# The carried state of four early units, run chunk by chunk through its own copy, and a new order for the words around it

## The chip, the cores and the metric

The kernel runs on one core of a Trainium2 chip. The metric is the device time of one execution in microseconds. Times are the medians of several runs; a trace is of one profiled execution, whose own time stands beside its span below.

## The reference

Two parts follow each other. The first is a gated linear attention: for each of 4 batches and 8 heads a state of 48x48 runs over 768 steps.

```python
for t in range(S):
    state = alpha[:, :, t, :, None] * state + np.einsum('bhd,bhe->bhde', k[:, :, t], v[:, :, t])
    y[:, :, t] = np.einsum('bhd,bhde->bhe', q[:, :, t], state)
```

The second takes y as rows `x` of 3072 tokens by 384 and computes `silu(x @ w_gate) * (x @ w_val) @ w_out` with 1536 inner columns. The weights come in as doubles and are cut and split on the chip into a high and a low single-precision part.

## The kernel before, in words

The attention is cut into 16 **units** of 192 steps (`T`), four to a batch; units 0 to 3 are batch 0. A unit has 3 **chunks** of 64 steps (`NU`, `C`), and its 8 heads lie as 4 pairs (`G`), one head of a pair in partitions 0 to 63 and one in 64 to 127. The second part is cut into **steps**: block of 384 tokens by 128 inner columns. Step s has three products of nine matmuls each: `g` (gate, PSUM bank `gps`), `v` (value, bank `vps`) and `o` (output, three banks).

Everything is written as **words** in one table, `ORDER`. A word is `engine:name@banks`, with engines t (TensorE), v (VectorE, DVE), s (ScalarE, ACT), g (GpSimd, POOL) and y (the DMA queue of SP). Each engine carries out its words in the order of the table and waits where a word needs something that is not ready; nothing else orders the work. Digits after @ name the PSUM banks that the word writes.

The words of one unit u, as far as the change and the prediction speak of them:

- `La`, `Lq`, `Lk`, `V u.i`: loads of alpha, q, k and v. `pa`, `pq`, `pk` copy a load to a wide tile, `Ta`, `Tq`, `Tk` transpose it on TensorE, and `ea`, `cq`, `ek` copy it out of PSUM.
- `G`, `f`, `mk`, `q`: the scans over alpha and the products with k and q. `qc` copies a part of q's product.
- `K u.c` transposes a chunk of keys, `kc u.c` copies it into the tile `K` (two copies a chunk on ACT, lines 514 and 515).
- `S`: the scores (line 551), `ma u.i`: their masked copies. `Y`: the output of the unit (lines 629 to 646). `yh`, `yl` split it, `R u.k` rearranges it on TensorE and `x u.k` copies it to `xT`, from which step products read.
- `vc u`: a copy of v to the tile `U` for the second half of `Y`.
- `Bw u` (units 0 to 3) or `B u` (later units), function `carry`: what each chunk adds to the state. `ad u.c`, function `advance`: the state before the next chunk, written into free rows of the v tile `V`; for the last chunk it goes to `SE`. `de u`: VectorE multiplies `SE` by the decay and makes it the state ahead of the next unit's first chunk.

For the early units `Bw` makes whole sums: the state after chunk c is a sum of the products of chunks 0 to c, so that chunk 0 is multiplied once, twice and three times; the tile `K` holds an identity in the state rows of chunk 0, which brings in the state ahead of the unit. All three sums can then be made one after another with no copy between them.

Weights have words of their own: `wl p` (load), `w p v0` to `v2` (cut, ACT or DVE), `w p a` (high part) and `w p p` (low part). `sl s`, `h s`, `hh s`, `hl s` are the silu and the product between the matmuls of a step, `sl` on ACT. `first` is one 1x1 silu without any other use.

Of the kernel before, what the change touches and what calls it, by code (L numbers as in the profile page):

```python
# [48 lines left out]
s:pa2 y:V1.5 g:w1a v:w1p s:w4v0 y:La3 s:pa3 g:q1 v:de1 t:S1@62 t:Bw1@3 s:ad1.0 v:w2v2 g:w2a y:Lq2 v:w3v2 v:yl0.0
v:yl0.1 t:R0.1@7 g:qc1 v:ma1.0 v:ma1.1 v:w4v1 v:ma1.2 t:Ta2@05 s:ea2 v:G2 s:ad1.2 g:vc1 t:Y1@41 s:yh1.0 v:yl1.0  # L50
s:yh1.1 v:yl1.1 t:R0.0@2 s:x0.0 s:x0.1 y:Lk3 t:Ta3@35 y:Lk2 s:pk2 t:R0.2@6 v:w4v2 g:pq2 t:Tq2@04 s:cq2 v:lm1 t:R1.2@1
s:x1.2 s:x0.2 t:Tk2@72 v:mk2 t:R1.0@4 s:x1.0 v:f2 v:q2 t:R1.1@0 s:x1.1 t:K2.0@2 s:kc2.0 s:w4a v:w4p t:K2.1@7 s:kc2.1
s:w3a v:w3p g:w2p t:g0 s:sl0 t:K2.2@1 g:pk3 t:Tk3@40 s:ea3 v:G3 y:wl5 s:w5v0 v:w5v1 y:V2.3 y:V2.2 y:V3.1 y:V3.0
y:V3.3 y:V2.4 y:Lq3 s:pq3 y:V2.5 y:V2.1 y:wl7 y:V2.0 y:wl10 t:S2@27 t:g1 s:sl1 s:kc2.2 t:v0 v:h0 s:hh0 g:hl0 y:wl6
y:V3.2 y:V3.5 t:g2 s:vc2 t:Tq3@51 s:cq3 s:w7v0 s:sl2 g:lm0 y:La4 v:de2 t:Bw2@3 s:ad2.2 s:ad2.0 t:v1 v:mk3 v:ma2.2
t:K3.1@4 s:kc3.1 y:wl9 v:f3 v:q3 t:S3@16 s:w6v0 t:K3.0@3 s:kc3.0 g:qc2 v:ma2.0 v:ma2.1 t:Y2@42 s:yh2.0 y:V3.4 y:wl8
v:w5v2 s:w5a v:de3 t:Bw3@0 s:ad3.0 s:yh2.1 v:h1 s:hh1 v:w6v1 v:w6v2 v:yl2.0 v:ma3.2 g:qc3 v:ma3.0 v:yl2.1 y:wl12
y:wl11 y:xr2.0 y:Lk4 y:wl13 y:xr2.1 s:w6a v:w6p t:v2 v:h2 v:ma3.1 t:o0 g:w5p t:g3 t:v3 v:w7v1 s:w9v0 s:hh2 v:hl2
g:hl1 t:o1 t:o2 v:w7v2 s:w8v0 s:vc3 y:wl14 v:w8v1 t:K3.2@1 v:w9v1 v:w8v2 s:sl3 v:h3 s:w7a v:w7p v:w9v2 s:w8a v:w8p
s:w10v0 v:w10v1 s:w9a v:w9p t:Y3@20 s:yh3.0 t:g4 s:sl4 s:hh3 g:hl3 s:yh3.1 v:yl3.1 t:v4 v:h4 v:yl3.0 y:xr3.1 y:xr3.0  # L60
y:xr3.2 y:xr2.2 y:wl16 t:g5 s:w11v0 v:w11v1 v:w10v2 t:v5 s:sl5 v:h5 s:hh4 v:hl4 v:w11v2 s:w10a v:w10p t:o3 t:o4
s:w12v0 v:w12v1 s:hh5 v:hl5 v:w12v2 s:w11a v:w11p s:w12a g:w12p v:tk4 t:g6 t:v6 s:sl6 v:h6 s:hh6 g:hl6 v:tr4 v:G4
y:V5.2 y:Lq4 y:V4.2 t:o5 t:g7 s:sl7 s:kc3.2 s:w13v0 t:v7 v:h7 t:o6 s:ot6.1 y:V4.4 y:os6.1 s:ot6.0 y:os6.0 y:La5 v:mk4
v:w13v1 v:f4 s:w14v0 s:hh7 g:hl7 y:wl15 y:V5.0 y:V4.1 y:V4.0 y:wl17 t:g8 s:sl8 t:v8 v:h8 s:hh8 g:hl8 v:w14v1 t:g9
s:w16v0 v:tq4 s:ot6.2 s:sl9 t:v9 v:h9 v:w13v2 t:o7 v:w14v2 s:w14a g:w14p v:q4 v:tr5 t:g10 t:v10 s:sl10 y:V5.4 s:w13a
v:h10 s:hh10 v:kr4.2 v:kr4.0 t:o8 s:hh9 v:hl9 s:w15v0 v:w15v1 v:w13p v:w16v1 t:g11 t:v11 s:sl11 v:h11 t:o9 g:hl10
t:o10 v:w15v2 s:w15a s:hh11 g:hl11 v:G5 t:g12 t:v12 v:kr4.3 s:sl12 v:h12 s:w17v0 s:hh12 t:g13 s:sl13 v:w16v2 g:hl12
t:v13 t:o11 t:o12 y:Lk5 y:os6.2 v:tk5 g:mk5 v:w15p v:kr4.1 v:h13 s:hh13 y:V4.5 y:V4.3 y:Lq5 g:hl13 s:qc4 s:w16a v:f5
t:g14 v:tq5 g:q5 g:w16p v:w17v1 y:wl18 s:sl14 t:v14 v:h14 s:hh14 g:hl14 t:S4@21 v:ma4.2 t:B4@0 v:ma4.1 v:kr5.0 t:o13
s:ot13.0 s:ot13.1 s:vc4 v:kr5.1 y:os13.0 s:ad4.0 v:ad4.1 v:ma4.0 t:g15 s:sl15 t:v15 v:h15 s:w18v0 v:w18v1 t:g16  # L70
s:sl16 s:ot13.2 s:hh15 g:hl15 v:w17v2 s:w17a g:w17p v:w18v2 s:w18a g:w18p t:v16 v:h16 v:ad4.2 y:La6 v:tr6 t:g17 t:v17
s:sl17 v:h17 t:o14 t:o15 y:V5.1 y:Lk6 v:tk6 v:kr5.2 s:hh17 g:hl17 v:kr5.3 t:Y4@56 s:yh4.0 s:yh4.1 v:yl4.0 v:yl4.1
y:V5.3 y:V5.5 v:G6 v:mk6 t:S5@10 t:B5@2 v:kr6.2 v:kr6.1 t:g18 s:sl18 t:v18 t:g19 s:hh16 g:hl16 t:o16 t:o17 y:Lq6
# [1036 lines left out]
```

## Time and profile before

| | |
|---|---|
| median of 3 runs | 553.8 us (553.6 to 554.41) |
| profiled execution | 553.2 us, span 551.5 us |
| TensorE busy | 537.0 us (97%) |
| VectorE busy | 383.9 us (70%) |
| ScalarE busy | 257.7 us (47%) |
| GpSimd busy | 134.4 us (24%) |

Busy time on TensorE (PE in the rows) is the time in which a matmul is under way. Idle time of another engine costs nothing unless TensorE or the last store waits for it. The shares are means over the whole span; the change lies in its first third, where ScalarE and VectorE are much fuller than these means.

### The profile page before, as it was taken

Reading aid. Unit: us, or ns where it says so; the run is one execution under the profiler, and the core shown is the slowest. Engines: PE = TensorE matmul, PEld = TensorE weight load, DVE = VectorE, ACT = ScalarE, POOL = GpSimd, SP = SyncE. Lnnn points to the kernel's source line nnn. Section 1 sums busy time; section 2 is a strip of 40 time slices with the busy share of each in tenths; the row PEclk is TensorE's granted clock in tenths of the full one; section 3 lists DMA queues with packets and bytes.
Section 4 is the critical chain, followed back from the end, with each engine's and each line's share of the span. In section 5 each row is a group of like instructions: output and inputs, shape, how many; then the busy total and the mean of one; then the engine's idle time right before and its main releaser. Section 6 shows DMA issues by size and latency. Waiting matters only on the chain.

```text
span 551.5 us, 13702 instructions
## 1 busy us (share of the span) xinstructions
PE 537.0 (97%) x5510; PEld 524.5 (95%) x5510; DVE 383.9 (70%) x612; ACT 257.7 (47%) x581; POOL 134.4 (24%) x146
## 2 busy tenths in 40 slices
PE   5999999999999999999999999999999999999996
...
GB/s 253 192 233 283 250 153 256 139 81 152 166 155 217 142 125 161 82 112 86 102 106 188 142 73 171 145 86 159 74 168 36 65 40 91 84 125 115 131 174 115
DMA packets 95362, 77.61 MB, mean 141 GB/s; under 512 B 32832, under 2 KB 92224, under 8 KB 95296
## 3 DMA queue, kind: packets, MB, share of 16 engines
...
q10 hardware_dynamic: 288, 0.39, 0.2%
...
## 4 chain that ended last, share of the span: by engine, by line
PE 87%; DVE 4%; SPq 3%; ACT 2%; DMA 2%; issue 2%; DVEq 0%; ACTq 0%
PE v L715 25%; PE g L715 25%; PE ops L747 24%; PE A L575 3%; PE y L646 2%; PE s L551 2%; PE pt L416 1%; PE y L629 1%; SPq L700 1%; DMA Le<-in_k_dram 1%; PE y L630 1%; PE kps L510 1%; DMA L<-in_k_dram 1%; DVE Gs L460 1%; DVE K L526 1%
## 5 line engine op out<-in xcount | busy, mean ns | idle before, releaser
L715 PE MATMUL g<-xT,w 128*128 128x384 f32 x864 | 167.5, 337 | 0.6 <-issue 0.6
L715 PE MATMUL v<-xT,w 128*128 128x384 f32 x864 | 166.8, 337 | 0.3 <-DVE h L727 0.3
L747 PE MATMUL ops<-w,hh 128*128 128x384 f32 x576 | 157.3, 336 | 0.0
L715 PEld LDWEIGHTS g<-xT,w 128*128 128x128 f32 x864 | 150.9, 188 | 1.9 <-issue 0.9
L715 PEld LDWEIGHTS v<-xT,w 128*128 128x128 f32 x864 | 150.9, 188 | 1.4 <-DVE h L727 0.8
L736 POOL TENSOR_TENSOR hl<-h,hh 128x384 fp32r<-128x384 f32 x63 | 67.5, 1073 | 309.5 <-ACT hh L731 279.5
L727 DVE TENSOR_TENSOR h<-h,v 128x384 f32<-128x384 f32 x96 | 53.1, 553 | 103.3 <-PE v L715 94.5
L731 ACT CAST hh<-h 128x384 fp32r<-128x384 f32 x96 | 49.0, 513 | 141.4 <-DVE h L727 69.5
L747 PEld LDWEIGHTS ops<-w,hh 128*128 128x128 f32 x576 | 105.3, 188 | 0.2
L747 PE MATMUL ops<-w,hl 128*128 128x384 f32 x288 | 96.8, 336 | 0.0
L723 ACT ACTIVATE h<-g 128x384 f32<-128x384 f32 x96 | 47.0, 490 | 77.4 <-PE g L715 66.5
L526 DVE STREAM_TRANSPOSE K<-Gs 32x384 f32<-32x384 f32 x96 | 54.7, 570 | 1.9
L747 PEld LDWEIGHTS ops<-w,hl 128*128 128x128 f32 x288 | 54.1, 188 | 0.1
L736 DVE TENSOR_TENSOR hl<-h,hh 128x384 fp32r<-128x384 f32 x33 | 18.8, 575 | 24.0 <-ACT hh L731 23.9
L469 DVE TENSOR_TENSOR_SCAN AT<-AT,back 128x771 f32<-128x771 f32 x16 | 32.6, 2037 | 0.6
L585 DVE TENSOR_TENSOR X<-s,mask 64x384 f32<-64x384 f32 (+1 forms) x48 | 26.1, 552 | 6.2 <-PE s L575 3.2
L460 DVE TENSOR_TENSOR_SCAN Gs<-AT,inj 128x772 f32<-128x772 f32 x16 | 28.8, 1803 | 0.4 <-ACT AT L811 0.2
L660 ACT CAST X<-y 112x384 fp32r<-112x384 f32 x28 | 12.5, 478 | 32.3 <-PE y L646 26.5
L664 DVE TENSOR_TENSOR X<-y,X 112x384 fp32r<-112x384 f32 x28 | 15.2, 552 | 14.1 <-ACT X L660 13.9
L317 ACT ACTIVATE wc<-wc,wbias 128x384 f32<-128x384 f32 x36 | 23.3, 648 | 1.2
L575 PE MATMUL A<-V,K 64*48 64x48 f32 (+1 forms) x720 | 22.0, 207 | 1.8 <-issue 1.8
L575 PEld LDWEIGHTS A<-V,K 64*48 64x48 f32 (+1 forms) x720 | 19.4, 123 | 2.6 <-issue 1.8
...
## 6 DMA issues: line engine op xcount, KB each, us to landing
...
```

The lines of the kernel that those rows point to most:

```text
L317: nc.scalar.activation(dev, dev, AF.Relu, bias=wbias, scale=-1.0, accum_out=wviol[:, 0, i : i + 1])
L460: nc.vector.tensor_tensor_scan(*(x.rearrange("p g t -> p (g t)")[:, ::-1] for x in (Gs, AT, inj)), 0.0, op0=ALU.mult, op1=ALU.add)
L469: nc.vector.tensor_tensor_scan(Af, Af, back[:, 1 : n + 1], back[:, 0:1], op0=ALU.mult, op1=ALU.add)
L526: nc.vector.transpose(out=bass.AP(k0.tensor, k0.offset, [k0.ap[0], (G * 2 * D, NU), (2 * D, G), (1, 32)]), in_=Kg[j * BO + x : j * BO + x ...
L575: nc.tensor.matmul(to[j * BO : j * BO + D, g - gs.start, :], Ks[r, x, g, KC[j]], Vd[r, x, g, VC[j]], start=(x == 0 or not whole), stop=(x ...
L585: nc.vector.tensor_tensor(out=X[r, z, f * GF : (f + 1) * GF, :].rearrange("r g (c t) -> r g c t", c=NU), in0=sps[f][r].rearrange("r g (c t ...
L715: nc.tensor.matmul(pt, wsp[kind, f][a][:, kt * P : (kt + 1) * P], xT[blk][:, b_, kt, :], start=(n == 0), stop=(n == 3 * KT - 1),)
L723: nc.scalar.activation(h, acc.pop(("g", blk, f)), AF.Silu)
L727: nc.vector.tensor_tensor(out=h, in0=h, in1=acc.pop(("v", blk, f)), op=ALU.mult)
L731: nc.scalar.copy(out=hh, in_=acc["h", blk, f])
L736: eng.tensor_tensor(out=hl, in0=acc.pop(("h", blk, f)), in1=hh.bitcast(F32), op=ALU.subtract)
L747: nc.tensor.matmul(ops[blk][i], h[b_][:, i * P : (i + 1) * P], wsp["o", f][a], start=(first and n == 0), stop=(last and n == 2),)
```

## The change

`Bw` is gone. In its place stand three words `C u.c` a unit (two for unit 3), function `running`: one product per pair and half, 8 a chunk. The tile `K` now holds the identity in the state rows of every chunk, so the product of chunk c takes the state from the rows where `ad u.(c-1)` has put it. `ad u.c` is now a word for every chunk (in the table before, `ad u.0` copied two chunks at once). A unit has 24 products where it had 48.

```diff
-            nc.gpsimd.tensor_copy(out=t_[r, 0, :, KC[j]], in_=ident[r, r].unsqueeze(1).to_broadcast([D, G, D]))
+            nc.gpsimd.tensor_copy(out=t_[r, :, :, KC[j]], in_=ident[r, r].unsqueeze(1).unsqueeze(1).to_broadcast([D, NU, G, D]))
...
+    def running(u, c, bank):
+        st = state[u]
+        Ks, Vd = st["K"], st["V"]
+        st["sum"] = ps.tile([P, G, D], F32, tag=bank, name=f"A2_{u}_{c}")
+        for g in range(G):
+            for j in range(2):
+                r = slice((1 - j) * BO, (1 - j) * BO + C) if c == 0 and first_of_batch(u) else slice(0, P)
+                nc.tensor.matmul(
+                    st["sum"][j * BO : j * BO + D, g, :], Ks[r, c, g, KC[j]], Vd[r, c, g, VC[j]], start=True, stop=True
+                )
...
     def advance(u, c, eng):
...
+        if "sum" in st:
+            for j in range(2):
+                r = slice(j * BO, j * BO + D)
+                to = Vd[r, c + 1, :, VC[j]] if c + 1 < NU else SE[r]
+                (eng.copy if eng is nc.scalar else eng.tensor_copy)(out=to, in_=st["sum"][r])
+            return
...
-        todo[f"Bw{u}"] = lambda eng, bank: carry(u, bank, True)
+        for c in range(NU):
+            todo[f"C{u}.{c}"] = lambda eng, bank, c=c: running(u, c, bank)
```

The table `ORDER` is new down to word `h25` (some 640 words); from there both tables agree. Its first line of old and of new:

```diff
-s:first y:La0 y:wl0 s:pa0 t:Ta0@20 s:ea0 y:La1 s:pa1 y:Lq0 s:pq0 y:Lk1 y:Lk0 t:Ta1@67 s:pk0 v:w0v0 v:w0v1 v:w0v2 s:w0a g:w0p
+y:La0 v:pa0 t:Ta0@53 s:ea0 y:wl0 v:w0v0 v:w0v1 v:w0v2 y:Lq0 s:pq0 v:G0 v:f0 t:Tq0@41 v:q0 y:La1 s:pa1 y:Lk1 s:pk1
```

Besides the order, some words change engine. Ahead of step 0, ACT gains `qc0`, `w1a` and `w2a` (POOL had them) and gives `w2v0`, `pa0` and `pa2` to DVE; `w3a` now stands ahead of the last `x` copies of unit 1 and `w4a` behind the first silu, where both stood between those copies and the silu. After it ACT gains `qc2`, `qc3` and `pk3` and gives `w7v0` and `w10v0` to DVE, while DVE gives `w6p` and `w9p` to POOL. `first` moves from the head of ACT's words to far behind the first silu.

**TensorE, unit 1.** Before, the words S1, Bw1 and R0.1 stand together (s_1 is the scores' tile, A_1 and a part of s_1 take the state sums, xp is unit 0's rearranged output):

```order
L551 MATMUL s_1_446<-X_103,Gs_212 64x64 x2
L551 MATMUL s_1_447<-X_103,Gs_212 64x64 x2
L575 MATMUL A_1_472<-V_81,K_104 48x48 x24
L575 MATMUL s_1_446<-V_81,K_104 48x48 x12
L575 MATMUL A_1_472<-V_81,K_104 48x48 x12
L686 MATMUL xp_1_531<-Y_428,sel_121 128x384 x2
```

In the changed kernel the same place reads (A_1_0, A_1_1 and A_1_2 are the sums of the three chunks; the rows of S1 are left out, and y_1 is the word Y1):

```order
L589 MATMUL A_1_0_410<-V_81,K_104 48x48 x8
L417 MATMUL pt_0_0_434<-ident,wide 128x128 x3
L417 MATMUL pt_0_1_438<-ident,wide 128x128 x3
...
L589 MATMUL A_1_1_472<-V_81,K_104 48x48 x8
L589 MATMUL A_1_2_487<-V_81,K_104 48x48 x8
L648 MATMUL y_1_512<-X_103,V_81 64x64
```

48 products have become 3 times 8, and the last two groups stand side by side with nothing between them, though the third needs ACT's copy of the second.

**ScalarE around the first silu.** Before (kps are key transposes, t3 and t4 cut weights, h0_0 the silu of step 0):

```order
L514 COPY K0_104<-kps2_1_670 64x4x48
L515 COPY K0_104<-kps2_1_670 64x4x48
L340 CAST w3_677<-t3_276 128x768
L723 ACTIVATE h0_0_691<-g0_0_681 128x384
L811 COPY AT_85<-pt3_0_0_606 128x4x32x3
L811 COPY AT_85<-pt3_0_1_610 128x4x32x3
L160 ACTIVATE t5_714<-raw5_711,lbias_119 128x768
L404 COPY wide_82<-L1_72 128x12x48
L723 ACTIVATE h0_1_770<-g0_1_760 128x384
```

And in the changed kernel:

```order
L516 COPY K0_104<-kps2_1_644 64x4x48
L742 ACT_TABLE_LOAD
L742 ACTIVATE h0_0_664<-g0_0_654 128x384
L341 CAST w4_669<-t4_502 128x768
L830 COPY AT_85<-pt3_0_0_565 128x4x32x3
L830 COPY AT_85<-pt3_0_1_569 128x4x32x3
L492 COPY X0_102<-X0_102 48x384
L515 COPY K0_104<-kps2_2_679 64x4x48
L516 COPY K0_104<-kps2_2_679 64x4x48
L405 COPY wide_82<-L1_72 128x12x48
L161 ACTIVATE t5_700<-raw5_589,lbias_119 128x768
L742 ACTIVATE h0_1_702<-g0_1_686 128x384
```

A table load has come in ahead of the first silu, and between the silus of steps 0 and 1 stand three more words: `w4a` (line 341), `qc2` (492) and `kc2.2` (515 and 516). In both programs one more table load stands at the very head of ACT's work.

## Rows read from the trace of the kernel before

**Rows 1.** The page: busy us, share, instructions; TensorE's busy tenths in 40 slices
```profile
PE 537.0 (97%) x5510; PEld 524.5 (95%) x5510; DVE 383.9 (70%) x612; ACT 257.7 (47%) x581; POOL 134.4 (24%) x146
...
PE   5999999999999999999999999999999999999996
```

**Rows 2.** Stretches A:B: length, then busy us of PE, PEld, DVE, ACT, POOL; granted clock
```profile
5.00:10.00 5.00, 3.53 (x16) 3.16 (x17) 4.16 (x6) 2.37 (x5) 3.90 (x8) 1.00 0.99 304
...
20.00:25.00 5.00, 4.21 (x142) 3.46 (x142) 4.94 (x10) 4.81 (x14) 1.94 (x2) 1.00 0.79 193
25.00:30.00 5.00, 4.43 (x134) 4.10 (x137) 3.59 (x7) 4.24 (x10) 2.57 (x6) 1.00 0.69 184
30.00:35.00 5.00, 5.00 (x68) 4.44 (x61) 4.72 (x9) 4.86 (x13) 2.85 (x2) 1.00 0.77 199
```

**Rows 3.** Chain that ended last, 34 to 66 us: start, us, what
```profile
35.51 1.58 PE g L715 x9
...
37.47 0.66 PE pt L416 x6
38.13 0.86 PE s L551 x48
...
44.59 1.21 PE A L575 x48
45.80 0.54 PE s L575 x24
46.34 0.54 PE A L575 x24
...
52.08 1.22 PE A L575 x48
...
64.95 1.07 PE g L715 x5
```

**Rows 4.** Groups of instructions by shape: count, then busy us, mean ns
```profile
L340 ACT CAST w<-t 128x768 fp32r<-128x768 f32 x16 | 13.2, 834 | 10.5 <-DVE t L164 10.5
...
L491 ACT COPY X<-X 48x384 f32<-48x384 f32 x9 | 4.6, 510 | 0.2
...
L598 ACT COPY V<-A 48x384 f32<-48x384 f32 x8 | 3.8, 474 | 0.8 <-PE A L575 0.7
...
L404 ACT COPY wide<-L 128x576 f32<-128x576 f32 x5 | 3.4, 681 | 0.0
...
L160 ACT ACTIVATE t<-raw,lbias 128x384 f32<-128x384 uint32 x3 | 1.9, 647 | 0.0
L605 ACT COPY V<-A 48x192 f32<-48x192 f32 x6 | 1.9, 313 | 3.4 <-PE A L575 3.4
L605 ACT COPY SE<-A 48x96 f32<-48x96 f32 x6 | 1.4, 233 | 0.1
...
L340 ACT CAST w<-t 128x384 fp32r<-128x384 f32 x2 | 1.0, 511 | 2.8 <-DVE t L164 2.8
```

**Rows 5.** ScalarE in order of time: start, us, what [idle before <-releaser]
```profile
15.50 0.31 ACT L514 COPY K<-kps 64x192 f32<-64x192 f32 x1 [0.50 <-PE kps L510]
...
27.52 0.97 ACT L598 COPY V<-A 48x384 f32<-48x384 f32 x2 [0.66 <-PE A L575]
...
33.42 1.74 ACT L690 CAST xT<-xp 128x384 fp32r<-128x384 f32 x4
...
37.85 0.48 ACT L723 ACTIVATE h<-g 128x384 f32<-128x384 f32 x1
...
40.81 0.49 ACT L723 ACTIVATE h<-g 128x384 f32<-128x384 f32 x1 [0.17 <-PE g L715]
```

**Rows 6.** ScalarE, the first two instructions, same columns
```profile
0.91 1.28 ACT L897 ACT_TABLE_LOAD   x1 [0.91 <-PEq L1094]
2.20 0.20 ACT L897 ACTIVATE first<-one 1x1 f32<-1x1 f32 x1
```

**Rows 7.** TensorE in order of time, early transposes, same columns
```profile
7.98 2.82 PE L416 MATMUL pt<-ident,wide 128*128 128x128 f32 x12 [1.19 <-ACT wide L404]
```

More of the change, by code (lines that the diff above doesn't have):

```diff
@@ L49 @@
[L49 to L73, printed above, removed]
@@ new lines @@
+t:S0@24 t:K0.2@7 v:ma0.2 s:ek1 s:kc0.0 s:qc0 s:kc0.1 s:kc0.2 y:wl3 s:w3v0 y:V0.1 y:V0.3 y:V0.0 y:V1.4 y:V0.4 y:La2
+y:wl2 y:V0.2 y:V0.5 y:V1.3 y:Lq2 y:V1.1 t:Tq1@17 t:C0.0@6 v:mk1 v:w0p s:cq1 v:f1 g:q1 g:qc1 s:ad0.0 t:K1.0@0 t:K1.2@3
+s:kc1.0 t:C0.1@5 s:ad0.1 t:C0.2@6 t:K1.1@7 v:ma0.1 v:ma0.0 s:vc0 t:Y0@40 v:w2v0 v:pa2 y:V1.2 y:La3 y:V1.0 y:wl4 y:Lk3
+y:V1.5 s:ad0.2 v:de1 t:C1.0@2 s:kc1.2 s:kc1.1 s:yh0.0 s:yh0.1 v:w1v2 v:w2v1 s:ad1.0 v:w3v1 v:w2v2 s:w1a t:Ta2@31 s:ea2
+g:w1p v:w3v2 t:S1@57 t:C1.1@2 s:ad1.1 v:ma1.2 s:pa3 y:V2.0 y:V2.2 t:C1.2@7 y:V2.4 y:V2.1 y:Lk2 y:wl6 s:w4v0 s:w2a
@@ new lines @@
+s:ad1.2 v:ma1.1 v:ma1.0 g:vc1 t:Y1@61 s:yh1.0 g:pq2 s:yh1.1 v:yl0.1 v:yl0.0 t:R0.2@4 t:R0.0@2 s:x0.2 s:x0.0 t:Ta3@53
+s:pk2 t:Tq2@47 s:cq2 g:w2p y:V3.1 y:V3.0 y:V3.2 y:wl5 t:R0.1@2 s:x0.1 y:Lq3 y:wl9 y:V2.5 y:wl8 y:V2.3 v:G2 v:yl1.0
+v:yl1.1 v:w4v1 v:w4v2 t:R1.1@0 t:Tk2@47 v:mk2 s:x1.1 t:R1.2@6 v:f2 t:R1.0@2 s:w3a s:x1.2 s:x1.0 s:pk3 t:K2.0@4
+t:K2.1@7 s:kc2.0 s:kc2.1 v:q2 t:g0 s:sl0 v:de2 v:w3p s:w4a t:Tk3@17 t:K2.2@0 s:ea3 t:g1 s:qc2 s:kc2.2 s:pq3 s:w5v0
+s:sl1 y:wl7 y:V3.4 y:wl12 y:V3.3 y:V3.5 v:w4p v:G3 t:v0 v:h0 s:hh0 g:lm0 g:hl0 t:S2@02 t:C2.0@4 s:ad2.0 v:w5v1 v:ma2.2
@@ new lines @@
+v:mk3 t:g2 t:C2.1@1 s:sl2 s:ad2.1 t:Tq3@24 s:cq3 v:f3 v:q3 t:C2.2@7 s:ad2.2 t:K3.1@3 s:kc3.1 s:vc2 v:de3 v:ma2.0
+v:ma2.1 t:K3.0@6 s:kc3.0 t:v1 t:S3@17 t:C3.0@3 t:Y2@06 s:w6v0 s:ad3.0 s:qc3 v:w5v2 s:w5a g:w5p v:w6v1 v:h1 t:C3.1@2
+s:hh1 v:w6v2 s:w6a g:w6p s:yh2.0 s:yh2.1 s:vc3 v:ma3.2 v:lm1 v:ma3.1 v:w7v0 t:v2 v:hl1 t:o0 t:o1 v:h2 v:ma3.0 s:ad3.1
+t:Y3@21 y:wl11 y:wl13 y:V4.4 y:wl10 y:wl16 v:yl2.1 v:yl2.0 y:xr2.0 y:xr2.1 y:xr2.2 v:w7v1 v:w7v2 s:w9v0 s:w8v0 s:hh2
+v:w8v1 v:hl2 y:V4.2 y:Lk4 s:w7a t:g3 t:v3 t:o2 s:sl3 v:w8v2 v:w7p s:w8a t:g4 v:w9v1 v:h3 v:w9v2 s:w11v0 s:yh3.0
```

155 lines of the change are left out of this document (83 added, 72 removed).

## The prediction

> **What bounds the kernel now.** I read the page first. TensorE is busy 537.0 of the 551.5 us of the span, and its row of slices shows a 9 everywhere but in the first slice and the last [rows 1]. The kernel is a line of matmuls with a thin start; what is taken off TensorE there counts in full where the line is dense, and nothing where another engine sets the pace. So I looked at the start by stretches. From 20 to 30 us TensorE is busy 4.21 and 4.43 of each 5 us, from 30 on all 5.00; ScalarE in the same three stretches is busy 4.81, 4.24 and 4.86, VectorE 4.94, 3.59 and 4.72 [rows 2]. Up to about 35 us three engines are equally full, and a saving on TensorE alone need not arrive. The chain that ended last goes through matmuls alone from 35.51, the first step product, to 64.95, where g4 starts [rows 3]: there TensorE is the bound. ScalarE in order of time shows how units 0 and 1 end: the last four copies into xT, from which g0 reads, take 1.74 from 33.42 and end at 35.16 [rows 5]. The reader should see that g0 at 35.51 stands right behind both a full TensorE and a full ScalarE.
>
> **What the products save.** Bw2 is 96 records (a product leaves two) and takes 1.21 + 0.54 + 0.54 = 2.29 us; Bw3 is 48 records and takes 1.22 [rows 3]. The changed unit 2 has 48 records; at the price of the 48 of line 575 that is 1.21, in three groups of 0.40. Unit 3 has 32 records, 0.81. So units 0, 1 and 2 save 1.08 each and unit 3 saves 0.41, together 3.65 us of TensorE, 2.16 of it ahead of g0 and 1.49 behind it.
>
> **What the copies cost.** Before, ad of a unit is four copies of 48x96 to SE (0.233 each) and two of 48x384 (0.474): 1.88 us of ScalarE. After, it is six of 48x192 (0.313): 1.88 us [rows 4]. The copies are even; what changes is that each now stands between two products. GpSimd's wider identity copy at the start is before any product needs it and is costed at nothing; uncovered, it would be two copies of three times the size, some 1.5 us by ScalarE's 48x384 copy of 0.510 [rows 4].
>
> **Ahead of g0 (units 0 and 1).** Here I go by ScalarE, because its copies free the banks and fill the tiles. It gains qc0 (0.510), w1a and w2a (0.511 each) and w3a (0.834) ahead of the last xT copies, 2.37 us. It loses w2v0 (0.647) and pa2 (0.681), 1.33 [rows 4]. Net it has 1.04 more. In the old trace it idles 0.50 in front of the key copies at 15.50 and 0.66 in front of the state copies at 27.52 [rows 5], 1.16 in all. qc0 falls into the first gap. The second came from waiting for the end of Bw1; in the new order other words (w1a, then ea2; pa3, w4v0, w2a) stand between one state copy of unit 1 and the next, which are longer than the product of 0.40 with its own delay, so ScalarE doesn't wait. It ends the xT copies 0.12 earlier, near 35.0. TensorE does wait, between C1.1 and C1.2: the copy ad1.1 stands behind w1a (0.51) and ea2 (two copies of 128x384, by the pair at 27.52 some 0.97) and takes 0.63 itself, 2.11 in all, of which C1.1 covers 0.40 and S1 some more; about 1.2 us are left, half of the 2.16. The other half goes into waits for the state copies of unit 0. So this part gives -0.1 (bounds: -0.7 if ScalarE's gaps and a part of its overlap vanish, since TensorE then leads again; +1.5 if each of the unit's three state copies is late by half a microsecond).
>
> **Between g0 and g4 (units 2 and 3).** TensorE is dense, so 1.49 come off in full. Against it stand three new waits.
>
> First, the table load. `first` is moved behind the first silu, and the new ScalarE order has a load ahead of h0_0. Its row of before is 1.28 us [rows 6]. From 35.0 ScalarE has pk3 (0.681), four key copies (0.31 each by [rows 5]), the load and the silu (0.48): 35.0 + 0.68 + 1.24 + 1.28 + 0.48 = 38.7. g1 needs that silu, because it writes the bank that g0 filled. TensorE does g0 (1.58), Tk3 (0.66) and K2.2 (0.39) from 35.5 and is ready at 38.1 [rows 3]: a wait of 0.6 to 0.8; I take 0.7. Uncovered it would be 1.28, wholly covered 0.
>
> Second, the silu of step 1, on which g2 waits. Between the first two silus ScalarE took 40.81 - 37.85 = 2.96, with 0.17 of it idle [rows 5]. It now has w4a (0.834), qc2 (0.510) and kc2.2 (0.62) more: 2.79 + 1.96 = 4.75 from 38.2, so the silu ends at 43.4. TensorE does g1, v0 (1.57 each by g0's row), S2 (0.86) and C2.0 (0.40) from 38.8 and is ready at 43.2: 0.2 to 0.6, I take 0.4 (0 to 1.0).
>
> Third, unit 2's chunks: C2.2 waits for ad2.1, which waits for C2.1 and stands behind a silu of 0.49. Tq3 (0.66) covers most of it; 0.3 remains. In unit 3, Y2 and step products lie between the two groups, and I cost it at nothing; bare, one copy of two pieces (0.63) would show.
>
> Sum: -0.1 - 1.49 + 0.7 + 0.4 + 0.3 = **-0.2 us**. The profiled execution's span of 551.5 would become 551.3, its own time 553.2 become 553.0; the median of the runs stands 0.6 above that execution, so I forecast **553.6 us**.
>
> VectorE gains pa0, pa2, w0p, w2v0, w7v0 and hl1 and loses w1p, w6p and w9p up to g4. It had 1.41 us idle in 25 to 30 alone [rows 2], and I cost the difference at nothing; if that cover were gone, three casts of weights on the way to a step product would be late, which is part of the upper bound.
>
> **A rule of the skill on the table load.** The row at 0.91 is followed by its silu at 2.20, 0.01 behind the load's end: at the head of the program a load costs its own 1.28 and no more [rows 6].
> The Trainium skill (ScalarE: Activation LUTs, section What ACT_TABLE_LOAD costs) says that a switch of tables costs the load of about 1283 ns and on top of it a drain of about 1380 ns, 2.66 us together; the trace agrees on the load and, with nothing in front of it, shows no drain.
> By the row the sum is -0.2. By the page it would be an estimated +1.2, since g1 would wait 1.4 longer and little behind it could take that up.
>
> **The rivals.** Faster: the waits are covered, because matmuls start piece by piece as chunks get ready and ScalarE overlaps its ends. Then at least the 1.49 stay, at most all 3.65: 552.3 to 550.2, I would name 551.9. For it speaks that the old trace has hardly a wait on TensorE behind 30 us; against it that ScalarE is as full as TensorE there and that the load stands on its line. It decides when the first silu ends before 38.1.
>
> Slower: the load on ScalarE's line. A switch in the middle of the program must let the work in front of it end, and then both silus come later. If another length of the load is added, g1 waits 2.0, not 0.7: +1.1, 554.9, and 555.3 with the upper half of the other two waits. It decides when the first silu starts later than 39.0. For it: nothing stands between load and silu to cover it. Against: the old row shows 1.28 alone. The page of the Trainium skill named above (ScalarE: Activation LUTs, What ACT_TABLE_LOAD costs) would make it the likelier case.
>
> Slower too: TensorE's pace. The early transposes take 2.82 for 12 at 7.98, after an idle 1.19, and 0.66 for 6 at 37.47, at a granted clock that the rows give as 1.00, the 2.4 GHz level, from 5 to 10 us as from 20 on [rows 2, 3, 7]. If the new pauses bring that slow pace back for 5 us, the 4.21 us of work of the stretch from 20 to 25 would be half done, +2.1: 555.7. The pauses are shorter than 1.5 us each, so I give it little. That the change doesn't do what it says is out: the program has the 24 products.
>
> **How the numbers follow.** The forecast, saving and waits in balance (552.7 to 554.8): 0.47. Covered waits: 0.31. Longer load: 0.16. Pace: 0.06. Below 0.2% (1.1 us) this kernel's runs, which spread over 0.8, tell little. So faster 0.31, same 0.47, slower 0.22. The range reaches to the nearer part of the faster rival and through the load's: 551.8 to 555.2, which leaves about 0.1 on each side.
>
> **What would show it.** In the changed profile: 48 records of line 589 in unit 2 taking about 1.2; a load of 1.28 between the key copies and the first silu near 37, and g1 waiting for that silu by some 0.7; g2 for the next by 0.4; C1.2 waiting for a state copy by about 1; the first step product at 35.5. Wrong would be: g0 at 34 or at 37, a load of 2.6, or idle TensorE behind g4, which none of these terms has.

## The result: slower by about one per cent

The changed kernel takes 560.65 us (557.58 to 562.37, four runs) for 554.11 beside it, a ratio of 1.0112 with an interval of 1.0067 to 1.0158. Run again on another occasion it took 559.49 for 554.14, 1.0093 (1.0076 to 1.0111). The forecast was 553.6, its range 551.8 to 555.2.

The profiled execution took 562.37, its span is 560.7, 9.2 more than before. The page, with the rows that answer to [rows 1], and the row of the granted clock:

```profile
PE 539.2 (96%) x5350; PEld 522.2 (93%) x5350; DVE 392.9 (70%) x613; ACT 256.9 (46%) x582; POOL 142.2 (25%) x147
...
PE   4799999999999999999999999999999999999996
...
PEclk9979999999999999999999999999999999999999
```

TensorE has 160 records fewer, as the change promised, and yet 2.2 us more busy time; VectorE has 9.0 us more. The third slice, from 28 to 42 us, has a 7 in the clock's row. Three of the stretches of [rows 2]:

```profile
20.00:25.00 5.00, 4.63 (x126) 3.87 (x130) 4.88 (x10) 4.76 (x15) 1.77 (x2) 1.00 0.74 199
25.00:30.00 5.00, 2.79 (x95) 2.53 (x91) 4.91 (x8) 4.25 (x10) 3.23 (x3) 0.81 0.94 264
30.00:35.00 5.00, 5.00 (x74) 4.62 (x72) 2.54 (x5) 2.04 (x5) 2.27 (x3) 0.51 0.63 150
```

From 30 to 35 us TensorE runs at the 1.2 GHz level, half of what [rows 2] show there. What it did just before, in order of time:

```profile
26.80 0.26 PE L589 MATMUL A<-V,K 128*48 128x48 f32 x2 [0.57 <-DVE X L598]
28.70 0.77 PE L589 MATMUL A<-V,K 128*48 128x48 f32 x13 [1.64 <-DMA V<-in_v_dram]
```

C1.2 waits for the load of V1.5, the last piece of unit 1's values. The chain that ended last goes through that load (start, us, what):

```profile
22.85 5.72 DMA V<-in_v_dram
...
28.70 0.77 PE A L589 x13
...
32.31 1.58 PE xp L705 x4
33.89 1.23 PE pt L417 x6
...
40.87 1.28 ACT L742
42.16 0.50 ACT h L742
...
42.70 1.83 PE g L734 x9
```

The six transposes take 1.23 here and 0.66 in [rows 3]. The first step product starts at 39.02 by the rows in order of time, for 35.28 before (35.51 in the chain). From there to the silu of step 26, where the two orders of words have become the same, I took the whole stretch, called the middle stretch from here on (columns as above). Of before it is

```profile
35.28:178.66 143.38, 143.38 (x1544) 140.31 (x1542) 135.66 (x200) 73.54 (x145) 44.65 (x37) 1.00 0.69 188
```

and of after

```profile
39.02:188.46 149.44, 144.98 (x1475) 138.80 (x1476) 141.36 (x198) 72.41 (x145) 53.74 (x43) 1.00 0.63 172
```

So the 9.2 us are 3.7 ahead of the first step product and 6.1 behind it, with 0.6 back in the equal rest. The 6.1 are the larger part, and there the clock is 1.00. TensorE, which had no idle time in this stretch, now has 4.46; the list of its waits over the whole span says for whom above all (total, times, longest; one of the seven lies behind the stretch):

```profile
PE ops L766 <- DVE hl L755: 2.2, 3, 1.1
...
PE v L734 <- DVE h L746: 1.8, 4, 0.6
```

Of the 4.46 us, 3.63 are six waits for VectorE (`h`, `hl`), whose busy time in the stretch grew by 5.7 us. That growth is not work. VectorE near 60 us and at 73, in order of time:

```profile
59.42 2.18 DVE L755 TENSOR_TENSOR hl<-h,hh 128x384 fp32r<-128x384 f32 x1
...
73.05 2.49 DVE L173 SCALAR_TENSOR_TENSOR t<-raw,t 128x768 uint32<-128x768 uint32 x1
```

and GpSimd at the same time:

```profile
57.05 4.14 POOL L345 TENSOR_TENSOR w<-t,w 128x768 fp32r<-128x768 f32 x2 [8.18 <-ACT w L341]
...
72.56 2.17 POOL L345 TENSOR_TENSOR w<-t,w 128x768 fp32r<-128x768 f32 x1
```

`hl` takes 0.55 elsewhere and the weight step 0.95. Both start while GpSimd works on a two-input row and end 0.4 and 0.8 us after it. The middle stretch has three more such rows of VectorE: 2.60 at 123.39 and 1.75 at 132.72 for 0.95, 1.56 at 174.03 for 0.55. Together the five are 6.6 us longer than elsewhere, more than the whole growth of 5.7, and each of the six waits comes behind one of them, with VectorE not idle in between. In the middle stretch of before the longest row of these kinds is 1.03. The second trace of the changed kernel (e17 below) has the same five, of 1.56 to 2.63.

### The profile page after: what moved, and what is told of

Same layout as the page of the kernel before. It is cut to its first block, busy times and chain, and to the rows that moved or that the text cites. A ratio compares the mean times of both kernels' runs of the same rounds, so it can differ in the third digit from the quotient of the medians.

```text
span 560.7 us, 13379 instructions
## 1 busy us (share of the span) xinstructions
PE 539.2 (96%) x5350; PEld 522.2 (93%) x5350; DVE 392.9 (70%) x613; ACT 256.9 (46%) x582; POOL 142.2 (25%) x147
## 3 DMA queue, kind: packets, MB, share of 16 engines
q1 hardware_dynamic: 95008, 76.32, 51.3%
## 4 chain that ended last, share of the span: by engine, by line
PE 74%; DVE 14%; DMA 5%; issue 3%; ACT 2%; SPq 2%; DVEq 0%; ACTq 0%
PE v L734 22%; PE g L734 22%; PE ops L766 22%; PE y L665 2%; PE A L576 2%; DVE Gs L461 2%; PE s L552 2%; DVE AT L470 1%; DMA L<-in_q_dram 1%; DMA L<-in_alpha_dram 1%; DVE K L527 1%; DMA V<-in_v_dram 1%; DVE X L598 1%; PE y L649 1%; DVE t L176 1%
## 5 line engine op out<-in xcount | busy, mean ns | idle before, releaser
L755 DVE TENSOR_TENSOR hl<-h,hh 128x384 fp32r<-128x384 f32 x33 | 21.3, 647 | 23.6 <-ACT hh L750 23.4
L345 POOL TENSOR_TENSOR w<-t,w 128x768 fp32r<-128x768 f32 (+1 forms) x13 | 23.7, 1824 | 25.6 <-ACT w L341 22.0
L341 ACT CAST w<-t 128x768 fp32r<-128x768 f32 (+1 forms) x20 | 15.4, 771 | 12.2 <-DVE t L165 7.5
```

The costliest lines, as they stand in the source:

```text
L345: eng.tensor_tensor(out=lo, in0=src, in1=hi.bitcast(F32), op=ALU.subtract)
L755: eng.tensor_tensor(out=hl, in0=acc.pop(("h", blk, f)), in1=hh.bitcast(F32), op=ALU.subtract)
```

## The experiments

Eighteen more runs were made, one of them (e17) of the changed kernel itself. For each: the start of the first step product and of the silu of step 26 in its profiled execution (rows in order of time), and the ratio of its runs to those of the kernel before beside it.

| run | base | first step product | silu 26 | between | ratio (interval) |
|---|---|---|---|---|---|
| before | | 35.28 | 178.66 | 143.38 | 1 |
| after | | 39.02 | 188.46 | 149.44 | 1.0112 (1.0067 to 1.0158) |
| e17_again | after | 36.55 | 185.97 | 149.42 | 1.0093 (1.0076 to 1.0111) |
| e1_v15 | after | 37.22 | 186.61 | 149.39 | 1.0086 (1.0066 to 1.0106) |
| e2_first | after | 39.74 | 188.00 | 148.26 | 1.0102 (1.0082 to 1.0121) |
| e3_casts | after | 36.70 | 190.98 | 154.28 | 1.0131 (1.0111 to 1.0151) |
| e4_v0 | after | 37.44 | 189.22 | 151.78 | 1.0055 (1.0040 to 1.0071) |
| e5_three | after | 36.87 | 185.22 | 148.35 | 1.0053 (1.0030 to 1.0076) |
| e7_busy | after | 38.44 | 187.72 | 149.28 | 1.0141 (1.0114 to 1.0168) |
| e8_v1 | e5 | 35.83 | 184.51 | 148.68 | 1.0063 (1.0046 to 1.0080) |
| e10_h15 | e5 | 36.47 | 186.91 | 150.44 | 1.0123 (1.0093 to 1.0153) |
| e11_shift | e5 | 39.58 | 186.66 | 147.08 | 1.0133 (1.0108 to 1.0157) |
| e6_oldorder | before | 39.34 | 184.15 | 144.81 | 1.0015 (0.9997 to 1.0033) |
| e9_oldorder2 | before | 37.75 | 182.38 | 144.63 | 1.0029 (1.0014 to 1.0045) |
| e12_late | before | 39.70 | 182.70 | 143.00 | 1.0116 (1.0091 to 1.0141) |
| e13_pool | before | 36.56 | 186.12 | 149.56 | 1.0112 (1.0074 to 1.0150) |
| e14_v0 | before | 35.66 | 182.49 | 146.83 | 1.0053 (1.0030 to 1.0075) |
| e15_first | before | 35.59 | 180.49 | 144.90 | 1.0015 (0.9993 to 1.0037) |
| e16_units23 | before | 35.77 | 185.09 | 149.32 | 1.0015 (0.9987 to 1.0043) |
| e18_fill | before | 38.12 | 181.14 | 143.02 | 1.0015 (1.0001 to 1.0028) |

The rest behind the silu of step 26 is the same program in all and took between 370.4 and 374.8 us, so one profiled execution places a wait but doesn't price it; prices are taken from the ratios, 0.1% being 0.55 us.

**The late load and the clock.** First, the load alone.

```diff
-y:V1.0 y:wl4 y:Lk3 y:V1.5
+y:V1.0 y:V1.5 y:wl4 y:Lk3
```

> The changed kernel with one word moved on SyncE: the load of V1.5 is issued ahead of the two loads of wl4 and of Lk3, not behind them. Theory (the late load makes TensorE stop behind C1.1, and the stop brings the slow clock): the 1.64 us of waiting for the load go, the granted clock stays at 1.00 from 25 to 35 us, unit 1 ends at the pace of the kernel before, the first step product starts near 36 us for 39.02, and the time is some 3 us less than the 560.65 of the changed kernel: 557.5. Rival (the clock falls for another reason): only the wait goes, the windows 25 to 35 still show a clock near 0.5, 559. Rival (VectorE sets the pace from 51 us on anyway): the first step product is earlier and the end is not, 560.5.

The wait for the load is gone, and the clock stays up, from 30 to 35 us too:

```profile
30.00:35.00 5.00, 5.00 (x95) 4.44 (x96) 4.97 (x7) 4.74 (x12) 3.25 (x3) 1.00 0.96 289
```

But the first step product is at 37.22, not near 36, and the time is 559.53, not 557.5. The changed kernel run once more says why:

> The changed kernel itself once more, for a second trace and more times. Theory (when the load of V1.5 lands is chance, and with it the pause behind C1.1; the rest of the loss is fixed): 557.5 to 562.4 again. If in this trace the pause is under 1.5 us, the clock stays at 1.00 from 25 to 35 us and the first step product starts at 37 to 37.5; if it is over 2 us, half the clock from 28 us on and 39 or later. Behind it in either case 149 to 150 us to the silu of step 26. Rival (the pause and the clock have nothing to do with each other): a short pause with a low clock, or a long one without.

In that execution the load comes in time without any edit, although it is issued at 24.40 there and at 22.85 in the first trace. TensorE's wait at the same place:

```profile
28.35 0.74 PE L589 MATMUL A<-V,K 128*48 128x48 f32 x16 [0.99 <-ACT V L612]
```

and the stretches, with the clock:

```profile
25.00:30.00 5.00, 3.79 (x120) 3.23 (x114) 4.91 (x9) 4.89 (x12) 3.00 (x4) 1.00 0.54 111
30.00:35.00 5.00, 5.00 (x84) 4.43 (x80) 4.97 (x7) 4.76 (x13) 2.63 (x2) 1.00 0.93 251
```

So the late load is an event of some executions. It costs 2.5 us of the 3.7 where it happens (39.02 against 36.55), and at the median no more than 1.4 us (1.0086 against 1.0093 and 1.0112). Behind the first step product the two executions of the changed kernel agree to 0.02 us. Next, whether the pause makes the clock: work put into it in the changed kernel, then the late load put into the kernel before, bare and filled.

```diff
-t:C1.2@7
+t:D@7 t:C1.2@7        (e7; D: 16 transposes of ident into C1.2's bank; e18: 22, ahead of Bw1)
...
-s:pa2 y:V1.5 g:w1a ... s:pa3 g:q1
+s:pa2 g:w1a ... s:pa3 y:Lq2 y:Lk3 y:V1.5 g:q1        (e12 and e18, in the kernel before)
```

> The changed kernel with 16 transposes of the identity, 2.2 us of TensorE, put between C1.1 and C1.2, where it otherwise waits; their result is overwritten. Theory (it is the pause that lets the granted clock fall to half from 28 us on): the clock stays at 1.00 from 25 to 35 us though the wait for the load is no shorter, unit 1's end runs at the pace of before, the first step product starts near 36 to 36.5 us for 39.0, and the time is 558.5. Rival (the clock falls for what the stage does, not for the pause): windows 25 to 35 again below 1.00, 560.6 or, where the load comes early, up to 2.2 us more.

> The kernel before with one load later: V1.5 is issued behind Lq2 and Lk3, so that Bw1, which reads it, waits. Theory (a pause of TensorE of some 2 us or more at this place lets the granted clock fall, whatever the order): Bw1 waits 3 to 4 us from 25.5 us on, the clock shows half from about 28 us for several us, the stage to g0 runs at half pace there, and the time is 559 to 561 for 554.3. Rival (only the wait counts): the clock stays 1.00 from 25 to 40 us, and the time is 557.5 to 558.5.

> The kernel before with the late load of V1.5, as tried before, and 22 transposes of the identity (3 us, results overwritten) in front of Bw1, so that TensorE works while it would wait. Theory (the pause is what lowers the clock, not the late data): the load is as late, Bw1 ends as late, but the clock is 1.00 from 25 to 40 us, the first step product starts near 37.5 us for 39.7, and the time is 557 for 559.5. Rival (work without use heats or fills as the rest does, and the clock falls anyway, or the filling itself delays Bw1): 559.5 or more.

e7 shows nothing on the pause, since its load came early too: the clock is 1.00, the 2 us of added work delay unit 1, and the time is 562.39. The other two settle it. Late and bare, Bw1 waits, in order of time

```profile
29.45 0.51 PE L573 MATMUL s<-V,K 128*48 128x48 f32 x13 [3.63 <-DMA V<-in_v_dram]
```

and the stretch behind it is

```profile
30.00:35.00 5.00, 5.00 (x105) 4.32 (x100) 4.24 (x5) 2.87 (x9) 2.24 (x3) 0.66 0.72 222
```

Late and filled, in order of time and then by the same stretch:

```profile
24.57 2.62 PE L911 MATMUL extra<-ident 128*128 128x128 f32 x22
...
29.21 0.51 PE L573 MATMUL s<-V,K 128*48 128x48 f32 x13 [0.40 <-DMA V<-in_v_dram]
```

```profile
30.00:35.00 5.00, 5.00 (x106) 4.52 (x102) 4.95 (x8) 4.42 (x13) 3.21 (x2) 1.00 0.79 239
```

The load lands as late in both (29.4 and 29.2). Bare the kernel is 1.16% slower than before, filled 0.15%. The mean granted clock of the bare kernel's six runs is 0.989 to 0.997, of the filled one's twelve 0.998 to 1.000; the execution shown is the mildest of the six (557.44 of up to 562.4). It is the pause that lets the clock fall, and work of no use in its place saves 1.0%, 5.6 us.

**The table load.** Undone in the changed kernel, and put alone into the kernel before:

```diff
-y:La0 v:pa0 ... s:wc35 s:first v:h25
+s:first y:La0 v:pa0 ... s:wc35 v:h25        (e2; e15 is the reverse, in the kernel before)
```

> The changed kernel with the word first (the silu of one element) back at the head of ScalarE's list, as in the kernel before, so that the program has one table load. Theory (the second load costs what g1 waits): ScalarE's line is 1.28 us shorter ahead of the first silu, the 0.8 us of g1 go, 559.9. Rival (a switch costs a drain as well): more than 1.3 us go, 559.2 or less. Rival (VectorE or the late xT copies set the pace behind it): no change, 560.6.

> The kernel before with a third part alone: first, the silu of one element, stands behind wc35 and no longer at the head, so that a second table load comes ahead of the first silu. Theory (g1 waits for the silu by what the load is longer than its cover): a load of 1.28 us, the first silu 1 to 1.3 us later than at 37.85, g1 waits 0.5 to 1 us, 554.6. Rival (hidden): 553.8. Rival (load and drain, 2.7 us together): 555.5 or more.

The waits are as priced. In e15 ScalarE shows, in order of time,

```profile
38.26 1.28 ACT L721 ACT_TABLE_LOAD   x1
39.55 0.49 ACT L721 ACTIVATE h<-g 128x384 f32<-128x384 f32 x1
```

and TensorE

```profile
40.10 1.15 PE L713 MATMUL g<-xT,w 128*128 128x384 f32 x5 [0.80 <-ACT h L721]
```

In e2 the 0.8 us of g1 are gone and the middle stretch is 1.2 shorter. The times say less: for e15 0.15% with an interval that holds zero, and for e2 no change. In three of e2's four runs the mean granted clock was 0.993 or 0.994, and its trace has a pause of 2.08 in C1.2 with a clock of 0.50 from 30 to 35 us, so what it saved may have gone there.

**VectorE's work.** The first step of three weights, undone in the changed kernel, then put alone into the kernel before:

```diff
-v:w7v0 ... v:w10v0 ... v:w17v0
+s:w7v0 ... s:w10v0 ... s:w17v0        (e4; e14 is the reverse, each in front of its v1)
```

> The changed kernel with the first step of the weights w7, w10 and w17 (words w7v0, w10v0, w17v0) on ScalarE again, for VectorE. In this form VectorE has two instructions of 0.95 us for a weight, not three. Theory (VectorE is full from 51 to 90 us, and its three long instructions per weight are late for the casts and hidden values): it loses 3 to 4 us of work, the waits behind 60 us shrink by 1 to 1.5 us, 559.4. Rival (only the collisions with GpSimd count, not the work): 560.6. Rival (ScalarE, busy 2.9 of 5 us in 60 to 65, is late with the silus then): 561.5.

> The kernel before with another part of the new order alone: the first step of the weights w7, w10 and w17 on VectorE, for ScalarE (three instructions of VectorE for two, each in front of the weight's next). Theory (VectorE is full behind 50 us, and what is put on its line comes back as waits of TensorE for hidden values): 1.5 to 3 us slower, 556. Rival (VectorE has cover, as the prediction had it): 553.8.

This is the clearest pair. Taken out, the kernel is 0.38 to 0.57% faster (1.0055, against 1.0093 in e17 and 1.0112 at first), 2 to 3 us and more than expected; put into the kernel before alone, it is 0.53% slower, some 3 us. (e4's profiled execution, 561.9, is not typical: its other five runs took 557.4 to 557.9.) In e14 the clock is 1.00 up to the silu of step 26, VectorE's busy time in the middle stretch is 141.08 us for 135.66, and two waits of TensorE appear, in order of time, that the old trace lacks:

```profile
70.93 1.31 PE L713 MATMUL v<-xT,w 128*128 128x384 f32 x6 [0.72 <-DVE h L725]
...
125.59 0.62 PE L713 MATMUL g<-xT,w 128*128 128x384 f32 x2 [1.53 <-ACT h L721]
```

The three words themselves take 0.53 to 0.64 each, 1.7 of the 5.4 us. Nearly all the rest is two rows that start beside one of GpSimd's: a cast of 1.78 for 0.95 at 68.17, ahead of the first wait, and the step that follows w17v0, ahead of the second, VectorE's row first and then GpSimd's:

```profile
117.58 4.12 DVE L170 SCALAR_TENSOR_TENSOR t<-raw,t 128x768 uint32<-128x768 uint32 x1
...
117.24 1.86 POOL L483 TENSOR_TENSOR X<-trq,AT 112x768 f32<-112x768 f32 x1 [1.12 <-DVE trq L394]
119.06 1.83 POOL L342 TENSOR_TENSOR w<-t,w 128x768 fp32r<-128x768 f32 x1
```

The second wait is for ScalarE's silu, but ScalarE had itself stood 6.08 us for VectorE's h, which comes behind that row.

**GpSimd's casts.** VectorE's rows are long beside GpSimd's; are the casts moved to GpSimd the loss?

```diff
-g:w6p ... g:w9p ... g:w13p ... g:w15p
+v:w6p ... v:w9p ... v:w13p ... v:w15p        (e3; e13 is the reverse, in the kernel before)
```

> The changed kernel with the four casts w6p, w9p, w13p and w15p on VectorE again, for GpSimd. Theory (a VectorE instruction with both sources in SBUF that starts while GpSimd casts stands still until the cast is over: hl at 59.42 took 2.18 us for 0.55, and three of TensorE's waits for VectorE follow from such ones): VectorE gets 3.8 us of work, 0.95 each, and loses 6 to 7 us of standing still up to 135 us; the TensorE waits for hl and h of 1.05, 0.35, 0.66, 0.55 and 0.56 us shrink to 1 us together, and the time falls by 2 us to 558.6. Rival (VectorE is simply full there, and the long instructions are how the profiler books it): 3.8 us more of work make it worse, 562 to 564.

> The kernel before with one part of the new order alone: the casts w6p, w9p, w13p and w15p on GpSimd, for VectorE. Theory (VectorE's instructions that read two tiles from SBUF stand still while GpSimd casts, and cost more than the casts did): 0.5 to 1.5 us slower, 554.8 for the 553.8 of before. Rival (VectorE is relieved of 3.8 us and the standing still is covered): 553.5.

Moving them back is no cure: with the casts on VectorE the changed kernel is at 1.0131, no faster than at 1.0112 or 1.0093. (Its trace also has the pause of 2.84 in Y2 that is told below, with a clock of 0.87 from 50 to 60, so the 0.2 to 0.4% are no price of the casts.) The long rows at 59 and 73 are gone there, but the other three stay, a cast of 1.59 comes at 55.93, and VectorE has four casts more to do: its busy time in the middle stretch is 142.42 us, for 141.36. So e3 doesn't part VectorE's own work from its long rows. e13 missed its question, since w6p there stands in front of w5p in GpSimd's queue: w5p, which ran at 53.46 before, ends at 61.86, the step product behind it waits 3.68, and the clock falls to 0.66 from 60 to 70. It shows what a word put ahead of an urgent one costs, not what the long rows do.

**What is left of the new order.** The three edits above (V1.5, first, the weight steps) together, and on top of them two key transposes of unit 5 moved.

> The changed kernel with three parts undone at once: V1.5 is issued ahead of wl4 and Lk3, first stands at the head again, and w7v0, w10v0 and w17v0 are ScalarE's again. Theory (the parts add: 1.1 us for the load, nothing for the table load, 2.9 for VectorE's work, each against 560.65): 556.5. Rival (they are one queue: what is earlier at g0 only waits longer for VectorE behind 51 us): no better than without those three casts alone, 557.7. With all that, what is left above 554.7 is due to the rest of the new order.

```diff
-v:ad4.1 v:kr5.1 v:ad4.2 v:kr5.0 v:ma4.2 ... v:h16
+v:ad4.1 v:ad4.2 v:ma4.2 ... v:h16 v:kr5.1 v:kr5.0        (e10, on top of e5)
```

> As the kernel with three parts undone, with the key transposes kr5.1 and kr5.0 (2.3 us of VectorE together) moved from in front of h15 to behind h16. Theory (near 128 and 132 us TensorE waits 1.27 and 0.47 us because hidden values stand behind VectorE's work for unit 5, that is by the order of words): both waits go, and the time falls by 1.5 us to 555.4. Rival (VectorE is behind with everything there, with 9.7 of 10 us busy, and the wait moves on to h17 and the state products of unit 5): 556.9.

e5 took 556.92, 0.53% above the kernel before beside it. That is no less than with the weight steps alone undone (e4, 0.55%), so the parts do not add up, and the rival of the expectation holds. Five long rows of VectorE beside GpSimd are still in e5's trace, 5.0 us longer than elsewhere in all, and so are waits of TensorE for VectorE of 2.2 us and a wait of 1.99 in Y2, told next. In e10 the two waits that e5 has near 130 us, 1.27 and 0.47, became one of 1.70 for VectorE's h at 136.78: VectorE is busy 14.62 of the 15 us from 120 to 135 in e5, and reordering only names another waiter. (e10's time is higher than e5's, 1.0123; its trace has 2.83 of the wait told next and a clock of 0.84 from 50 to 60, which may be why.)

**A wait that no row names.** In ten of the traces Y2 stops for 0.6 to 2.8 us with "issue" as the reason. (The trace of before has one such wait of 0.59, in Bw1.)

```diff
-t:v1 t:S3@17 t:C3.0@3 t:Y2@06
+t:S3@17 t:C3.0@3 t:v1 t:Y2@06        (e8, on top of e5)
...
+t:D@0 t:Ta1@06        (e11, on top of e5: 12 small products, 24 records)
```

> As the kernel with three parts undone, and with the step product v1 moved from in front of S3 to behind C3.0, so that S3, C3.0 and Y2, 112 small records, no longer stand in one row. Theory (the wait of 0.7 to 2.8 us in the middle of Y2, which the rows call issue, is TensorE waiting for its next block of instructions, which comes over the same DMA engines as the weights): with 1.6 us of nine long records ahead of Y2 the wait is gone or under 0.3 us, no clock below 1.00 from 50 to 65 us, and the time is 0.5 to 1 us less than with v1 in its place: 555.8. Rival (it is a wait for data, or v1's later end makes h1, hh1 and o1 late): 556.5 to 557.5.

> As the kernel with three parts undone, with 12 small products of the identity (48x48, 24 records, results overwritten) put in front of Ta1 at the start, where TensorE idles. Theory (the wait in the middle of Y2 is for a block of instructions): the wait, so far in six kernels behind the same 25th record of its line, stands about 24 records earlier in the program now, at the start of that line's records or in those ahead of it, and again ends 2.5 us after the packet of the instruction queue. Rival (a wait for data): it stays behind the 25th record. The time is 556.9 either way.

TensorE in e5, in order of time:

```profile
52.65 0.31 PE L663 MATMUL y<-X,U 64*64 64x64 f32 x4
54.95 0.26 PE L663 MATMUL y<-X,U 64*48 64x64 f32 x2 [1.99 <-issue]
```

and in e11:

```profile
55.01 0.33 PE L663 MATMUL y<-X,V 48*64 48x64 f32 x2
55.90 0.26 PE L663 MATMUL y<-X,V 48*48 48x64 f32 x2 [0.56 <-issue]
```

The wait has moved from behind the 27th record of the line (the expectation had counted 25) to behind the 2nd, by 25 where 24 were added, though all data are the same. Its place goes with the place in the instruction stream. By the DMA view a packet of an instruction queue starts at 52.4 in e5 and at 53.3 in e11, and the products go on 2.5 and 2.6 us later; in e1, e2, e3, e4, e6, e8, e9 and e10 it is 2.5 to 2.7. Whether TensorE stands there goes by when the packet comes: in the second trace of the changed kernel it starts at 51.3, Y2 at 53.05, and no wait has a row; in e1, with the same TensorE words, it starts at 53.1, Y2 at 53.70, and TensorE stands 1.23. e8 shortened the wait to 0.61, but then S3 waited 0.66 for VectorE, and nothing was gained. e11's own time (1.0133, not e5's as expected) is no price of the wait: its 24 records took 2.15 us in the slow start, and the first step product came 2.7 later. The rest of the difference has no cause that was looked for.

**The products alone.** The old order with the new products, in two hand-made versions, and with them in units 2 and 3 only. (In e6 the last chunk of unit 0 is multiplied with unit 1's keys; the amount of work is the same.)

```diff
-t:Bw2@3 s:ad2.2 s:ad2.0 t:v1 ... t:K3.1@4 s:kc3.1
+t:C2.0@3 s:ad2.0 t:v1 t:C2.1@0 s:ad2.1 ... t:K3.1@4 s:kc3.1 t:C2.2@3 s:ad2.2
...
-t:Bw3@0 s:ad3.0 ... t:v2
+t:C3.0@0 s:ad3.0 ... t:v2 t:C3.1@0 s:ad3.1        (e16; e6 and e9 have the like in units 0 and 1)
```

> The new products alone: the kernel before with its own order of words, in which only the whole sums of units 0 to 3 are replaced by the running ones, C u.c with a copy ad u.c behind each; between two of a unit stands another product where the old order had one near (K1.2, K1.1, R0.1, Ta2, v1, K3.1), and w2v0 of ScalarE goes behind ad0.2. Theory (the saving arrives where TensorE is the bound, behind g0, and is lost ahead of it): 1.5 us less than before, 553.2 for its 554.7. Rival (all 3.65 us arrive): 551.0. Rival (each copy that now stands between two products makes TensorE wait, in eight places by 0.3 us or more): 555 to 557, and then the new products are the loss, not the new order.

> The new products in the old order once more, with the copies out of each other's way: C0.0 and its copy stand ahead of Tq1, K1.0, K1.1 and K1.2 follow the chunks of unit 0 in that order (in the first kernel of this kind a key copy of unit 1 came ahead of unit 0's last chunk, which so used unit 1's keys; the work was the same), the copies of unit 1 stand ahead of those of alpha and of the copy that waits for the load of alpha. Theory (the products save what they take off TensorE, if nothing waits): the first step product at 34 to 35.5 us, behind it 1 us less than before, 552.8 for its 554.3. Rival (ScalarE and VectorE, equally full, set the pace, and freed TensorE time is filled with waits too short for a row): 554.3. Rival (three copies on the way cost more than the products save, wherever they stand): 555.5 as the first of this kind.

> The kernel before, in its own order, with the new products for units 2 and 3 alone, which stand behind the first step product; units 0 and 1 keep their whole sums. Theory of the prediction (TensorE is dense there and what comes off counts in full): 3.51 us of whole sums become five groups of 0.4 to 0.49, that is 1.1 to 1.5 us less, 552.5. Rival (the copies between the products, and the block of instructions that Y2 waits for, take it back): 553.8 to 555.

None is faster. e9 is 0.29% slower and has these waits of TensorE, in order of time, ahead of the first step product at 37.75:

```profile
19.63 0.90 PE L587 MATMUL A<-V,K 128*48 128x48 f32 x16 [1.16 <-ACT V L610]
...
24.97 0.74 PE L587 MATMUL A<-V,K 128*48 128x48 f32 x16 [1.17 <-ACT Y L677]
27.63 0.91 PE L415 MATMUL pt<-ident,wide 128*128 128x128 f32 x6 [1.92 <-DVE Y L681]
```

e16, where all that is changed, but for GpSimd's wider identity copies at the start, stands behind the first step product, is at 555.18 for 554.1: the 1.1 to 1.5 us don't arrive, and a loss up to 0.43% is not excluded. In its trace o1 waits 2.36 for GpSimd's hl, and the clock is 0.83 from 60 to 70. (The wider copies cost nothing to be seen: its first step product is at 35.77, for 35.59 and 35.66 in e15 and e14, which don't have them.)

No kernel tried beats the kernel before.

## Why the prediction was wrong, step by step

**VectorE "at nothing" failed.** This is the main step. The record set the words that VectorE gains against those it loses, up to g4, with 1.41 us idle in 25 to 30 us as cover, while its own [rows 2] show 4.72 and 4.94 of 5 us in the stretches beside it. Its list is uneven too: w9p counts as lost, though it runs behind g4 in the changed kernel, while w10v0, which stands just ahead of it there, doesn't count as gained, and w17v0, which also goes to VectorE, is missing here and in the section on the change, as are w13p and w15p, which go to GpSimd. The three weight steps alone cost 2 to 3 us, shown from both sides (e4, e14). By amount the record was not far off: without the five long rows VectorE's busy time in the middle stretch would not have grown. What it had wrong is the wait: it weighed how much VectorE does and not when, and the new order and the moved words bring VectorE's rows beside GpSimd's, where five of them take 6.6 us more than elsewhere and TensorE waits 3.63 us behind them. That they are long because of GpSimd is read from where they start and end in three traces; no run removes them and nothing else. The record named "idle TensorE behind g4, which none of these terms has" as what would prove it wrong, and that is what the trace shows.

**"TensorE is dense, so 1.49 come off in full" failed.** The size first: a group of 16 records takes 0.49, not 0.40 (in the chain at 46.96), so unit 2 gives back 2.29 - 1.47 = 0.82 and unit 3 1.22 - 0.98 = 0.24, together 1.06. And not even these arrive (e16). A busy TensorE at 5.00 of 5 is not one that sets the pace: with 64 records less, its busy time in the middle stretch of after is 1.6 us longer, and in e6 and e9, in the old order, it is 143.29 and 143.26 for 143.38. Waits too short for a row, counted as busy, would explain that; no row shows them.

**Ahead of the first step product** ScalarE has no idle time from 11.6 to 28.9 us, as forecast for the two gaps of the old trace, and C1.2's wait, forecast as 1.2, is 0.99 where the load is in time. That the first step product then starts at 36.55 and not at 35.5 is a miss within the stated bounds (+1.5). What no bound held is V1.5: its load was issued at 20.84 before and 22.85 after, behind 768 KB of weights and Lk3, and the record priced no moved load. Where it is late, the first step product at 39.02 is past the 37 that the record named as a sign of being wrong.

**The rival of the pace** had the mechanism, with the wrong trigger (several pauses under 1.5 us) and too little chance. In the profiled execution it happened as described: 3.5 us later than the forecast's 35.5. At the median it is not the cause: e17's trace is free of it, and its runs are 0.93% slower all the same.

**The table load was right** as to length and wait. The forecast was 1.28, a silu right behind it and 0.7 of waiting by g1; measured are 1.28, 0.01 and 0.81, in e15 1.28, 0.01 and 0.80. That the wait costs time is not shown: the interval of e15 holds zero, and e2 and e5 gain nothing by its absence. The rival of the longer load is out: the silu follows the load's end at once, with ScalarE at work in front of the load.
The Trainium skill (ScalarE: Activation LUTs, section What ACT_TABLE_LOAD costs) adds a drain of about 1380 ns to the load's 1283; this case's rows agree on the load and show no such drain, in the middle of the program either.

**The waits of g2 (0.4) and C2.2 (0.3)** have no row; the copies are even, as said (0.64 for two, six of them 1.9).

The sum, in per cent of the kernel before, from single parts put into it: VectorE's weight steps 0.53, the products with their copies 0.29 (e9; 0.15 in e6 and e16), the table load 0.15, together 0.97, against 0.93 to 1.12 measured. That it comes out is in part luck: the intervals of the parts are 0.15 to 0.3 wide on each side, and from the other end it doesn't. With the weight steps, the table load and the late load all undone, 0.53 is left (e5, 0.30 to 0.76), where the products with their copies would leave 0.15 to 0.29. So about half of the loss is shown to be the weight steps on VectorE, and the rest belongs to the new products and the new order together, which no run parts.

Still open is how much VectorE's long rows beside GpSimd cost by themselves, and which pauses bring the clock down: e5 stood 1.99 us in Y2 and kept 1.00; the changed kernel stood 1.64 behind a first 0.57 and lost it, and so did e4 and e10 with 2.60 and 2.83 in Y2 (0.91 and 0.84 from 50 to 60 us).
